# The order of work at the head of a fused retention and gMLP kernel, and where its constants are made

## The chip, the cores and the metric

The kernel runs on one core of a Trainium2 chip. The metric is the device time of one execution in microseconds (us), as the median of several runs. The profile is that of one further execution, taken by the hardware profiler. The engines are named as the profile names them: PE is TensorE (matmuls and transposes; PEld its weight loads), DVE is VectorE, ACT is ScalarE, POOL is GpSimd, SP is SyncE, which here only issues DMAs.

## The reference

Eight sequences b of 576 positions, eight heads of 64. First a retention layer (attention without softmax, with a decay by distance), then a gated MLP in which positions are mixed by a 576 x 576 matrix:

```python
# retention
scores = q @ k.transpose(0, 1, 3, 2) / sqrt(64)
gamma = 1 - 2.0 ** (-5 - arange(8))                    # one decay for each head
Dmat = where(rel >= 0, gamma[:, None, None] ** rel, 0)  # rel = row position - column position
x = (scores * Dmat) @ v                                # -> [8, 576, 512], heads side by side
# gMLP
h = gelu_tanh(x @ w_in)                                # w_in: 512 x 1024
u, v = h[..., :512], h[..., 512:]
v_n = (v - mean(v)) / sqrt(var(v) + 1e-6) * g_ln
v_s = einsum('ts,bsd->btd', w_sg, v_n) + b_sg[None, :, None]
out = x + (u * v_s) @ w_out                            # w_out: 512 x 512
```

Inputs and output are float32 in the chip's main memory.

## The kernel before

**Blocks.** The decay of a head factors into a power of gamma at the row times one at the column (`gq`, `gk`), so q and k are scaled by tables and the mask is only causal. Retention then runs in chunks with a running state for each sequence. The work is cut into 18 blocks j. Blocks 0 and 9 hold the first 64 positions of four sequences each (two chunks of 128 rows, named MID in the second stage); every other block holds 256 positions of one sequence, two to a sequence (1 and 2 for sequence 0, 3 and 4 for sequence 1, and so on). `load(j)` issues the DMAs of k, q and v of a block: four pieces of 128 KB each for blocks 0 and 9, one DMA of 512 KB each for the others, on SyncE's queue (a few pieces of block 0 on ScalarE's). They go into a pool of three buffers.

**Units of a block.** `cast(j, part, engine)` scales and rounds k, q or v to bf16. `T(j, part)` transposes k or q on TensorE; `turn(j, part)` does that by a DMA on SyncE's queue, which in the main loop is how q gets transposed. `Sc` makes scores, which VectorE masks; `Z` and `firsts` make the running states; `inter` and `intra` add up the retention of a block, which ScalarE (or VectorE) copies out as `xT`. `V(j, c)` makes the v half of the gMLP for a chunk, gelu on ScalarE, and in the head hands its statistics out as four steps: `stats_of` (VectorE), `pow_of` (GpSimd, the power -0.5 of the variance), `cen_of` (VectorE) and `norm_of` (ScalarE, which writes `vn`). `U(j, c)` makes the u half, gelu on ScalarE. `W(b, c, half)` mixes positions, with five matmuls against the transposed `w_sg`, and VectorE multiplies by u. `O` is the output projection with its store.

**How b_sg is added.** The rows of a MID chunk leave half of the 128 partitions of each operand unused. `vnm`, the normed rows of MID, has 1.0 in that half, and `wL` has three rows there that hold b_sg, split into three bf16 parts by `split_b`; `place_b(e)` copies them in with three DMAs of 1.1 KB, and `clear_wL` zeroes the rest. `fill_consts` and `fill_first` write the 1.0s, on GpSimd: for one of its three buffers in the head, for the other two in the loop at block 5.

**Order.** The order is written out by hand, and each engine takes its instructions strictly in that order; waits between engines come from the data. Lines 657 to 782 are the head: blocks 0 to 2 and the setting up of the weights (`w_in` in two halves, cast in pieces on GpSimd and ScalarE; `load_w` for `w_sg` and `w_out` on GpSimd's DMA queue; `build_wT`, which transposes `w_sg` on TensorE and copies it out on VectorE), with `spin(n)`, n matmuls on zeros that keep TensorE's clock up. From line 788 on a loop runs over blocks 3 to 17: at block j it finishes block j (`quarters`, which also makes the scores of block j + 1), casts block j + 3, transposes block j + 2, loads block j + 4, and runs W and O units of finished sequences in between. Steps put off with `later` run some units on.

**SyncE's queue in the loop.** At block j there stand on it, in order, `more(q)` (q of block j + 4) and `turn(j + 2, "q")`, then k and v of block j + 4, with the stores of O units where these fall. Up to block 5 `more(q)` comes first, from block 6 on the transpose.

The lines that the steps below touch: 93 to 138 (set up, first loads), 161 to 187 (constants and b), 189 to 194 (loads of `w_sg`), 196 to 210 (`build_wT`), 254 to 271 (`cast`), 502 to 534 (the steps of V), 657 to 782 (head), 788 to 839 (loop).

Of the kernel before, what the change touches and what calls it, by code (L numbers as in the profile page):

```python
# [15 lines left out]
Alu = mybir.AluOpType  # L16
# [3 lines left out]
def kernel(  # L20
# [123 lines left out]
    def build_masks():  # L144
        nc.vector.tensor_copy(rel[:].rearrange("p a (b t) -> p a b t", b=2), rel_i[:])
        nc.vector.tensor_scalar(rel[64:], rel[64:], 128.0, None, op0=Alu.add)
        for n in range(2):
            nc.vector.tensor_scalar(mask[n][:], rel[:], 0.0, None, op0=Alu.is_ge)
        for c in range(2):
            nc.vector.memset(mask[1][64 * c:64 * c + 32].rearrange("p a (b t) -> p a b t", b=2)[:, :, :, 32:], 0.0)  # L150
# [10 lines left out]
    def clear_wL():  # L161
        nc.gpsimd.memset(wL[0][64:], 0.0)
        nc.gpsimd.memset(wL[1][:64], 0.0)
        nc.gpsimd.memset(wnat[:, :, 0:64], 0.0)
# [8 lines left out]
                rest = left  # L173

    def fill_consts():
        for x in (1, 2):
            nc.gpsimd.memset(vnm[x][0][64:], 1.0)
            nc.gpsimd.memset(vnm[x][1][:64], 1.0)

    def fill_first():  # L180
        nc.gpsimd.memset(vnm[0][0][64:], 1.0)
        nc.gpsimd.memset(vnm[0][1][:64], 1.0)

    def place_b(e):
        for n in range(3):
            r = 64 * (1 - e) + n
            nc.gpsimd.dma_start(wL[e][r:r + 1, :], bp[:SB * 2 - 1, n, :] if e else bp[1:, n, :])

    def load_w(j):
        if j == SB:  # L190
# [29 lines left out]
    def spin(n):  # L220
        for _ in range(n):
            nc.tensor.matmul(idle[:], fill[:, :128], fill[:], start=True, stop=True)
# [177 lines left out]
    def Z(j, c):  # L400
        weave(z_steps(j, c))
# [89 lines left out]
    def V(j, c, wait=(2, 5)):  # L491
        p, m = chunk(j, c)
        hv = psD.tile([128, F2], F32, name="hv", tag="d")
        for kk in range(KK):
            nc.tensor.matmul(hv[:], xT(p, m)[:, kk], w_in[:, kk, F2:],  # L495
                             start=(kk == 0), stop=(kk == KK - 1))
        vg = vgp.tile([128, F2], F32, name="vg")
        nc.scalar.activation(vg[:], hv[:], Act.Gelu_apprx_tanh)  # L498

        st = both_of.setdefault(j, {}) if wait else {}  # L500
        k, n = (c, 2) if wait else (0, 1)

        def power():
            nc.gpsimd.tensor_tensor(st["rs"][:], st["rs"][:], mhalf[:, :n], op=Alu.pow)  # L504

        def stats():
            bst = w3.tile([128, 6], F32, name="bst")
            nc.vector.bn_stats(bst[:], vg[:])  # L508
            if not k:
                st.update(mv=w3.tile([128, n, 2], F32, name="mv"), rs=w3.tile([128, n], F32, name="rs"))  # L510
            nc.vector.bn_aggr(st["mv"][:, k], bst[:])
            if k == n - 1:
                nc.vector.tensor_scalar(st["rs"][:], st["mv"][:, :, 1], 1e-6, None, op0=Alu.add)  # L513
            if wait:
                if k:
                    power()
                centre()

        def centre():
            vc = w2.tile([128, F2], F32, name="vc", bufs=3)  # L520
            nc.vector.scalar_tensor_tensor(vc[:], vg[:], st["mv"][:, k, 0:1], g_bc[:], op0=Alu.subtract, op1=Alu.mult)  # L521
            st[k, "vc"] = vc

        def norm():
            rs, vc = st["rs"][:, k:k + 1], st[k, "vc"]
            if m == MID:
                for e in range(2):
                    half = slice(64 * e, 64 * e + 64)
                    nc.scalar.mul(vnm[p % 3][e][half], vc[half], rs[half])
                vns[p, m] = vnm[p % 3]  # L530
            else:
                vn = vnp.tile([128, F2], BF, name="vn")
                nc.scalar.mul(vn[:], vc[:], rs)  # L533
                vns[p, m] = [vn, vn]

        if wait:
            later(wait[0], stats)
            st[c] = norm
            if c:
                late = late_of.get(j, 1)  # L540
                later(wait[1] + late, st[0])
                later(wait[1] + late + 1, st[1])
        else:
            parts = stats, power, centre, norm
            for d, f in zip((stats_of, pow_of, cen_of, norm_of), parts):
                d[2 * j + c] = f
        tick()
# [109 lines left out]
    HEAD = 3  # L657
    spin(16)
    build_masks()
    cast(0, "k", nc.vector)  # L660
    T(0, "k")
    spin(2)
    cast(0, "q", nc.vector)
    T(0, "q")
    spin(3)
    cast(0, "v", nc.gpsimd)
    clear_wL()
    Sc(0, 0)
    Sc(0, 1)
    firsts(0)  # L670
    nc.gpsimd.tensor_copy(w_in[:, :2, F2:], w_stage[1][:, :2])
    nc.scalar.copy(w_in[:, 2:, F2:], w_stage[1][:, 2:])
    cast(1, "k", nc.gpsimd)
    spin(9)
    inter(0)
    intra(0)
    load(3)
    cast(1, "q", nc.vector)
    build_g()
    V(0, 0, None)  # L680
    V(0, 1, None)
    T(1, "k")
    T(1, "q")
    split_b()
    cast(1, "v", nc.gpsimd)
    spin(2)
    Sc(1, 0)
    Z(1, 0)
    stats_of[0]()
    cast(2, "k", nc.gpsimd)  # L690
    spin(2)
    inter(1)
    Sc(1, 1)
    Z(1, 1)
    load(4)
    cast(2, "q", nc.vector)
    spin(4)
    T(2, "k")
    spin(3)
    intra(1)  # L700
    T(2, "q")
    cen_of[0]()
    for j in range(SB):
        load_w(j)
    pow_of[0]()
    fill_first()
    cast(2, "v", nc.gpsimd)
    nc.gpsimd.tensor_copy(w_in[:, :, :256], w_stage[0][:, :, :256])
    V(1, 0, None)
    Sc(2, 0)  # L710
    V(1, 1, None)
    Z(2, 0)
    nc.scalar.copy(w_in[:, :, 256:F2], w_stage[0][:, :, 256:])
    inter(2)
    place_b(0)
    Sc(2, 1)
    firsts(1)
    start_state(1)
    wb = ["L0", "L1"] + list(range(SB - 1))
    U(0, 0)  # L720
    stats_of[2]()
    pow_of[2]()
    cen_of[2]()
    U(0, 1)
    stats_of[3]()
    pow_of[3]()
    intra(2)
    cen_of[3]()
    place_b(1)
    U(1, 0)  # L730
    V(2, 0, None)
    norm_of[2]()
    V(2, 1, None)
    load(5)
    norm_of[0]()
    stats_of[4]()
    pow_of[4]()
    cen_of[4]()
    build_wT(wb[0])
    U(1, 1)  # L740
    stats_of[5]()
    pow_of[5]()
    build_wT(wb[1])
    norm_of[3]()
    cen_of[5]()
    U(2, 0)
    cast(3, "k", nc.gpsimd)
    build_wT(wb[2])
    norm_of[4]()
    build_wT(wb[3])  # L750
    norm_of[5]()
    build_wT(wb[4])
    build_wT(wb[5])
    cast(3, "q", nc.vector)
    release(2)
    run(1)
    T(3, "k")
    cast(3, "v", nc.scalar)
    run(1)
    T(3, "q")  # L760
    U(2, 1)
    cast(4, "k", nc.gpsimd)
    cast(4, "q", nc.gpsimd)
    cast(4, "v", nc.scalar)
# [7 lines left out]
    T(4, "k")  # L772
    run(1)
    T(4, "q")
    run(1)
    cast(5, "q", nc.gpsimd)
    cast(5, "k", nc.gpsimd)
    cast(5, "v", nc.gpsimd)
# [9 lines left out]
    for j in range(HEAD, NB):  # L788
        nx = j + 1 < NB
        slots = where[share.get(j, 6)] if nx else (3, 0, 1, 1)  # L790
        more = (lambda *p: load(j + 4, p)) if j + 4 < NB else (lambda *p: None)
        if j < 6:
            more(q)
        if j + 2 < NB:
            turn(j + 2, "q")
            if j + 5 >= NB or j in EXTRA:
                turn(j + 2, "k")
        if j >= 6:
            more(q)

        if nx:
            quarters(j)
# [24 lines left out]
        if j + 3 < NB:  # L827
            cast(j + 3, "k", nc.gpsimd)
            cast(j + 3, "v", nc.gpsimd)
        if j == HEAD + 2:  # L830
            fill_consts()
        U(j, 1)
        if nx and place(j)[1] is not None and place(j)[2] == (place(j)[1] + 1 == GB) and place(j)[1] + 1 < B:
            start_state(place(j)[1] + 1)
# [41 lines left out]
```

## Time and profile before

| | |
|---|---|
| median of 3 runs | 219.12 us (218.86 to 222.0) |
| the profiled execution's own time | 219.96 us |
| its span, first to last instruction | 218.1 us |
| mean granted TensorE clock | 0.989 of full speed |
| busy share of the span | PE 92%, DVE 75%, ACT 59%, POOL 59% |
| DMA | 47.47 MB, 218 GB/s over the span |

The span is some 2 us shorter than the execution's own time, which also has start and end in it. A row of the profile in order of time gives the start in us, the length in us, the engine (with a q where it is the sequencer that issues a DMA), the line of the kernel, the operation, the tiles written and read, and how many instructions it stands for; in brackets stands how long the engine was idle before and what ended that. A row of a group gives the count, the busy time in us with the mean of one in ns, and the idle time before them. A DMA's row gives KB and the us from its issue to its landing.

### The profile page before, as it was taken

How to read it: one execution, taken by the hardware profiler on the slowest of the kernel's cores; microseconds unless marked ns; L12 is line 12 of the kernel's file. 1: busy time of each engine (PE TensorE's matmuls, PEld its weight loads, DVE VectorE, ACT ScalarE, POOL GpSimd, SP SyncE). 2: the span in 40 equal slices, each digit the busy share in tenths (PEclk: the TensorE clock that was granted, in tenths of full speed). 3: DMA queues.
4: the chain of work that ended last, by engine and by line, in shares of the span. 5: the costliest groups of instructions: out<-in, count | busy, mean ns of one | idle time of the engine just before them, and what ended most of it. 6: DMA issues, size and time to landing. Idle time of an engine off the chain costs nothing.

```text
span 218.1 us, 7982 instructions
## 1 busy us (share of the span) xinstructions
PE 201.0 (92%) x3403; PEld 142.5 (65%) x3433; DVE 164.1 (75%) x342; ACT 128.3 (59%) x221; POOL 128.9 (59%) x146
## 2 busy tenths in 40 slices
PE   7797989899979999899899999999999999999990
PEld 2344567568747687658586876668776876667650
DVE  5557869989957989856856779657866997968771
ACT  4354468564749777476568595777557374655100
POOL 5087978869895959856465747692957532111000
PEclk9999999979999999999999999999999999999998
DMA  6999999949999999999948999899999895532335
GB/s 155 254 312 291 335 243 286 290 109 295 198 278 248 282 213 182 278 182 340 247 111 131 335 242 216 196 267 315 198 276 201 201 125 136 155 101 48 144 93 200
DMA packets 88180, 47.47 MB, mean 218 GB/s; under 512 B 26000, under 2 KB 82640, under 8 KB 88144
## 3 DMA queue, kind: packets, MB, share of 16 engines
q1 hardware_dynamic: 85440, 45.10, 92.2%
q0 software_dynamic: 1472, 1.20, 3.3%
q10 hardware_dynamic: 1232, 0.66, 1.3%
q8 instruction: 27, 0.44, 0.9%
q14 instruction: 9, 0.07, 0.1%
HBM read 32.79 MB, written 9.44 MB: 194 GB/s over the span
## 4 chain that ended last, share of the span: by engine, by line
PE 63%; DVE 7%; DMA 4%; POOL 2%; issue 2%; ACT 1%; DVEq 0%; POOLq 0%; ACTq 0%
PE wp L586 15%; PE op L608 13%; PE hv L495 11%; PE hu L563 10%; DMA qT<-qb 4%; PE ot L479 3%; PE sc L345 3%; PE ot L437 2%; PE op L612 2%; PE tp L279 2%; DVE vc L521 2%; DVE qb L270 1%; DVE bst L508 1%; POOL rs L504 1%; POOL qb L270 1%
## 5 line engine op out<-in xcount | busy, mean ns | idle before, releaser
L349 DVE TENSOR_TENSOR ret<-sc,mask 128x512 bf16<-128x512 f32 x72 | 46.1, 682 | 14.6 <-PE sc L345 8.1
L504 POOL TENSOR_TENSOR rs<-rs,mhalf 128x2 f32<-128x2 f32 (+1 forms) x21 | 20.7, 987 | 55.5 <-DVE rs L513 55.3
L586 PE MATMUL wp<-wT,vn 128*128 128x288 bf16 x256 | 42.4, 289 | 0.9 <-DVE wT L252 0.9
L608 PE MATMUL op<-w_out,gT 128*128 128x512 bf16 (+1 forms) x131 | 34.8, 373 | 0.8
L563 PEld LDWEIGHTS <-w_in 128*128 128x128 bf16 x576 | 34.1, 98 | 1.9
L588 DVE TENSOR_TENSOR gT<-wp,uT 128x288 bf16<-128x288 f32 x64 | 27.5, 450 | 9.4 <-PE wp L586 9.0
L495 PE MATMUL hv<-w_in,xT 128*128 128x512 bf16 x119 | 31.9, 379 | 1.9 <-issue 1.0
L563 PE MATMUL hu<-xT,w_in 128*128 128x128 bf16 x512 | 33.6, 219 | 0.0
L508 DVE BATCH_NORM_STATS2 bst<-vg 128x6 f32<-128x512 f32 x36 | 24.7, 687 | 10.9 <-ACT vg L498 10.9
L270 POOL TENSOR_TENSOR kb<-qk,gk 128x1024 bf16<-128x1024 f32 x16 | 31.3, 1961 | 1.5 <-DMA qk<-in_k_dram 1.5
L498 ACT ACTIVATE vg<-hv 128x512 f32<-128x512 f32 x36 | 21.4, 597 | 14.7 <-PE hv L495 14.6
L586 PEld LDWEIGHTS <-vn 128*128 128x128 bf16 x256 | 24.1, 99 | 8.5 <-ACT vn L533 1.3
L521 DVE SCALAR_TENSOR_TENSOR vc<-vg,mv,g_bc 128x512 f32<-128x512 f32 x36 | 29.0, 805 | 0.6
L252 ACT CAST xT<-ot 128x512 bf16<-128x512 f32 x30 | 20.2, 741 | 14.2 <-PE ot L479 14.2
L270 POOL TENSOR_TENSOR qb<-qk,gq 128x1024 bf16<-128x1024 f32 x14 | 28.0, 1999 | 0.0
L566 ACT ACTIVATE uT<-hu 128x512 bf16<-128x512 f32 x32 | 19.1, 603 | 11.0 <-PE hu L563 11.0
L533 ACT ACTIVATE vn<-vc,rs 128x512 bf16<-128x512 f32 x32 | 22.4, 722 | 4.5 <-POOL rs L504 4.3
L608 PEld LDWEIGHTS <-gT 128*128 128x128 bf16 x148 | 13.3, 98 | 11.1
L495 PEld LDWEIGHTS <-xT 128*128 128x128 bf16 x128 | 11.8, 98 | 12.3 <-issue 1.3
L345 PE MATMUL sc<-qT,kT 64*64 64x128 bf16 x576 | 16.2, 219 | 2.7 <-DMA qT<-qb 1.6
L252 ACT COPY kT<-tp 128x1024 bf16<-128x1024 bf16 x15 | 15.2, 1010 | 6.0 <-PE tp L279 6.0
L586 PE MATMUL wp<-wL,vnm 128*128 128x288 bf16 x64 | 18.5, 289 | 0.0
(115 smaller groups left out, 294.2 us busy)
## 6 DMA issues: line engine op xcount, KB each, us to landing
qk<-in_k_dram SPq DMA_DIRECT2D x16, 512.0 KB, 6.7
qk<-in_q_dram SPq DMA_DIRECT2D x16, 512.0 KB, 7.0
vf<-in_v_dram SPq DMA_DIRECT2D x16, 512.0 KB, 7.5
out_dram<-ob SPq DMA_DIRECT2D x20, 256.0 KB, 4.7
out_dram<-obs SPq DMA_DIRECT2D x11, 256.0 KB, 2.4
wst<-in_moe_w_in_dram SPq DMA_DIRECT2D x2, 1024.0 KB, 7.4
vf<-in_v_dram SPq DMA_DIRECT2D x8, 128.0 KB, 4.7
out_dram<-ob SPq DMA_DIRECT2D x8, 128.0 KB, 2.8
```

What stands on the lines that cost most here:

```text
L252: (eng.copy if eng is nc.scalar else eng.tensor_copy)(o, i)
L270: eng.tensor_tensor(o, src, tab[:, kind].rearrange("p a h -> p h a").unsqueeze(3).to_broadcast([128, H, 2, D]), op=Alu.mult)
L345: nc.tensor.matmul(sc[r][cc, x, a, :], kT[rr, a, kk, cc], qT[rr, :, kk, cc], start=True, stop=True, skip_group_check=True)
L349: nc.vector.tensor_tensor(s["ret"][:, r, 2 * g:2 * g + 2], sc[r][:], mask[1 if place(j)[1] is None else 0][:].unsqueeze(1).to_broadcast([1 ...
L495: nc.tensor.matmul(hv[:], xT(p, m)[:, kk], w_in[:, kk, F2:], start=(kk == 0), stop=(kk == KK - 1))
L504: nc.gpsimd.tensor_tensor(st["rs"][:], st["rs"][:], mhalf[:, :n], op=Alu.pow)
L508: nc.vector.bn_stats(bst[:], vg[:])
L521: nc.vector.scalar_tensor_tensor(vc[:], vg[:], st["mv"][:, k, 0:1], g_bc[:], op0=Alu.subtract, op1=Alu.mult)
L563: nc.tensor.matmul(hu[:, c, :], w_in[:, kk, 128 * c:128 * c + 128], xT(p, m)[:, kk], start=(kk == 0), stop=(kk == KK - 1), skip_group_chec ...
L586: nc.tensor.matmul(ps[:], vns[p, m][e][:, 128 * c:128 * c + 128], w, start=(x == 0), stop=(x == SB - 1))
L588: nc.vector.tensor_tensor(gTs[p][:, c, col:col + HS], ps[:], uTs[b][:, c, half * HS:half * HS + HS], op=Alu.mult)
L608: nc.tensor.matmul(op[:], gTs[p][:, c, r], w_out[:, c, f], start=(c == 0), stop=(xn is not None and c == KK - 1), skip_group_check=True)
```

## The change

The head is put in another order and some work goes to other engines. In the order of the diff:

- `fill_consts` writes the 1.0s of all three buffers of `vnm` at once, on VectorE, ahead of the first cast; `fill_first` and the call in the loop go. `clear_wL` comes ahead of the casts, `split_b` ahead of the cast of v of block 0, both still on GpSimd. `place_b` issues its six DMAs on SyncE's queue, between the loads of blocks 3 and 4, not on GpSimd's.
- In `norm`, for MID chunks of the loop (block 9), one of the two halves is scaled on GpSimd, not on ScalarE.
- The numbers of idle matmuls (`spin`) are 34 in all, not 41.
- `build_g`, the scores and inner part of block 1, its V units, and the steps of the statistics come at other places; the loads of `w_sg` are issued in two parts, with the cast of v of block 2 between; the U units come at other places among the builds of the transposed `w_sg`.
- k of block 3 is cast on GpSimd further ahead, and q of block 3 on GpSimd, not on VectorE, also further ahead.
- U of block 2, second chunk, comes ahead of the first W unit, and one of the W units of the head moves to an earlier place.
- In the loop the transpose of q of block j + 2 comes ahead of the load of q of block j + 4 for blocks 3 to 5 too.

```diff
--- before.py
+++ after.py
@@ -173,18 +173,14 @@
                 rest = left
 
     def fill_consts():
-        for x in (1, 2):
-            nc.gpsimd.memset(vnm[x][0][64:], 1.0)
-            nc.gpsimd.memset(vnm[x][1][:64], 1.0)
-
-    def fill_first():
-        nc.gpsimd.memset(vnm[0][0][64:], 1.0)
-        nc.gpsimd.memset(vnm[0][1][:64], 1.0)
+        for x in vnm:
+            nc.vector.memset(x[0][64:], 1.0)
+            nc.vector.memset(x[1][:64], 1.0)
 
     def place_b(e):
         for n in range(3):
             r = 64 * (1 - e) + n
-            nc.gpsimd.dma_start(wL[e][r:r + 1, :], bp[:SB * 2 - 1, n, :] if e else bp[1:, n, :])
+            nc.sync.dma_start(wL[e][r:r + 1, :], bp[:SB * 2 - 1, n, :] if e else bp[1:, n, :])
 
     def load_w(j):
         if j == SB:
@@ -526,7 +522,10 @@
             if m == MID:
                 for e in range(2):
                     half = slice(64 * e, 64 * e + 64)
-                    nc.scalar.mul(vnm[p % 3][e][half], vc[half], rs[half])
+                    if e and wait:
+                        nc.gpsimd.tensor_scalar(vnm[p % 3][e][half], vc[half], rs[half], None, op0=Alu.mult)
+                    else:
+                        nc.scalar.mul(vnm[p % 3][e][half], vc[half], rs[half])
                 vns[p, m] = vnm[p % 3]
             else:
                 vn = vnp.tile([128, F2], BF, name="vn")
@@ -657,108 +656,112 @@
     HEAD = 3
     spin(16)
     build_masks()
+    clear_wL()
+    fill_consts()
     cast(0, "k", nc.vector)
     T(0, "k")
     spin(2)
     cast(0, "q", nc.vector)
     T(0, "q")
     spin(3)
+    split_b()
     cast(0, "v", nc.gpsimd)
-    clear_wL()
     Sc(0, 0)
     Sc(0, 1)
     firsts(0)
     nc.gpsimd.tensor_copy(w_in[:, :2, F2:], w_stage[1][:, :2])
     nc.scalar.copy(w_in[:, 2:, F2:], w_stage[1][:, 2:])
     cast(1, "k", nc.gpsimd)
-    spin(9)
+    spin(4)
+    build_g()
     inter(0)
     intra(0)
+    spin(3)
     load(3)
+    place_b(0)
+    place_b(1)
     cast(1, "q", nc.vector)
-    build_g()
     V(0, 0, None)
     V(0, 1, None)
     T(1, "k")
+    stats_of[0]()
     T(1, "q")
-    split_b()
     cast(1, "v", nc.gpsimd)
     spin(2)
     Sc(1, 0)
+    Sc(1, 1)
     Z(1, 0)
-    stats_of[0]()
+    pow_of[0]()
     cast(2, "k", nc.gpsimd)
+    spin(1)
+    inter(1)
+    Z(1, 1)
     spin(2)
-    inter(1)
-    Sc(1, 1)
-    Z(1, 1)
+    cen_of[0]()
+    intra(1)
     load(4)
     cast(2, "q", nc.vector)
-    spin(4)
+    spin(1)
     T(2, "k")
-    spin(3)
-    intra(1)
+    V(1, 0, None)
+    norm_of[0]()
+    for j in range(2):
+        load_w(j)
+    cast(2, "v", nc.gpsimd)
+    for j in range(2, SB):
+        load_w(j)
     T(2, "q")
-    cen_of[0]()
-    for j in range(SB):
-        load_w(j)
-    pow_of[0]()
-    fill_first()
-    cast(2, "v", nc.gpsimd)
+    Z(2, 0)
+    stats_of[2]()
+    V(1, 1, None)
     nc.gpsimd.tensor_copy(w_in[:, :, :256], w_stage[0][:, :, :256])
-    V(1, 0, None)
+    nc.scalar.copy(w_in[:, :, 256:F2], w_stage[0][:, :, 256:])
+    pow_of[2]()
     Sc(2, 0)
-    V(1, 1, None)
-    Z(2, 0)
-    nc.scalar.copy(w_in[:, :, 256:F2], w_stage[0][:, :, 256:])
+    Sc(2, 1)
     inter(2)
-    place_b(0)
-    Sc(2, 1)
     firsts(1)
     start_state(1)
     wb = ["L0", "L1"] + list(range(SB - 1))
     U(0, 0)
-    stats_of[2]()
-    pow_of[2]()
+    intra(2)
     cen_of[2]()
+    norm_of[2]()
     U(0, 1)
     stats_of[3]()
     pow_of[3]()
-    intra(2)
+    V(2, 0, None)
     cen_of[3]()
-    place_b(1)
-    U(1, 0)
-    V(2, 0, None)
-    norm_of[2]()
     V(2, 1, None)
     load(5)
-    norm_of[0]()
+    norm_of[3]()
     stats_of[4]()
+    cast(3, "k", nc.gpsimd)
     pow_of[4]()
+    U(1, 0)
     cen_of[4]()
-    build_wT(wb[0])
-    U(1, 1)
     stats_of[5]()
     pow_of[5]()
+    norm_of[4]()
+    U(1, 1)
+    cen_of[5]()
+    cast(3, "q", nc.gpsimd)
+    build_wT(wb[0])
+    norm_of[5]()
+    U(2, 0)
     build_wT(wb[1])
-    norm_of[3]()
-    cen_of[5]()
-    U(2, 0)
-    cast(3, "k", nc.gpsimd)
     build_wT(wb[2])
-    norm_of[4]()
     build_wT(wb[3])
-    norm_of[5]()
+    U(2, 1)
     build_wT(wb[4])
     build_wT(wb[5])
-    cast(3, "q", nc.vector)
     release(2)
     run(1)
     T(3, "k")
     cast(3, "v", nc.scalar)
     run(1)
     T(3, "q")
-    U(2, 1)
+    run(1)
     cast(4, "k", nc.gpsimd)
     cast(4, "q", nc.gpsimd)
     cast(4, "v", nc.scalar)
@@ -772,7 +775,6 @@
     T(4, "k")
     run(1)
     T(4, "q")
-    run(1)
     cast(5, "q", nc.gpsimd)
     cast(5, "k", nc.gpsimd)
     cast(5, "v", nc.gpsimd)
@@ -789,14 +791,11 @@
         nx = j + 1 < NB
         slots = where[share.get(j, 6)] if nx else (3, 0, 1, 1)
         more = (lambda *p: load(j + 4, p)) if j + 4 < NB else (lambda *p: None)
-        if j < 6:
-            more(q)
         if j + 2 < NB:
             turn(j + 2, "q")
             if j + 5 >= NB or j in EXTRA:
                 turn(j + 2, "k")
-        if j >= 6:
-            more(q)
+        more(q)
 
         if nx:
             quarters(j)
@@ -827,8 +826,6 @@
         if j + 3 < NB:
             cast(j + 3, "k", nc.gpsimd)
             cast(j + 3, "v", nc.gpsimd)
-        if j == HEAD + 2:
-            fill_consts()
         U(j, 1)
         if nx and place(j)[1] is not None and place(j)[2] == (place(j)[1] + 1 == GB) and place(j)[1] + 1 < B:
             start_state(place(j)[1] + 1)
```

## The prediction

> **What bounds the kernel now.** I read the shares of the page first, then the chain that ended last, then TensorE's waits, and last the 30 us around the place where they point.
>
> The page's table of engines, its TensorE row:
>
> ```profile
> PE 201.0 (92%) x3403; PEld 142.5 (65%) x3433; DVE 164.1 (75%) x342; ACT 128.3 (59%) x221; POOL 128.9 (59%) x146
> ```
>
> The chain in order of time (start, us, what), from where block 5 begins to matter, and one unit of each later kind:
>
> ```profile
> 42.39 2.81 DVE qb L270
> ...
> 46.28 0.89 PE hu L563 x16
> 47.17 0.40 PE sc L345 x16
> ...
> 50.45 1.94 POOL qb L270
> ...
> 52.67 8.80 DMA qT<-qb
> 61.52 0.63 PE sc L345 x30
> ...
> 65.77 0.45 PE tp L279 x8
> ...
> 73.08 0.86 PE hv L495 x4
> ...
> 76.90 0.61 PE wp L586 x5
> ```
>
> The longest of TensorE's waits after 60 us (who <- whom: us in total, times, longest):
>
> ```profile
> PE sc L345 <- DMA qT<-qb: 1.6, 1, 1.6
> ```
>
> The reader is to see two stages. From 61.52 on nearly every step of the chain is TensorE's. Before it the head is held by other things: the cast of q of block 3 on VectorE, that of q of block 5 on GpSimd, and the DMA that transposes the latter, for which TensorE waits 1.6 us. So the change, nearly all of it in the head, is worth what the score matmuls of block 5 (61.52) gain, as long as the later stream keeps up.
>
> What the DMA does meanwhile: SyncE's queue in order of time (start, length, what), and four stretches (length, then busy us of PE, PEld, DVE, ACT and POOL, granted clock, DMA share, GB/s):
>
> ```profile
> 21.86 2.00 SPq L88 DMA_DIRECT2D qk<-in_q_dram  x1
> 23.95 4.94 SPq L88 DMA_DIRECT2D vf<-in_v_dram  x1
> 29.00 3.40 SPq L88 DMA_DIRECT2D qk<-in_k_dram  x1
> ...
> 39.50 1.75 SPq L88 DMA_DIRECT2D vf<-in_v_dram  x1
> 47.01 0.37 SPq L88 DMA_DIRECT2D qk<-in_k_dram  x1
> ...
> 49.43 3.14 SPq L88 DMA_DIRECT2D qk<-in_q_dram  x1
> ```
>
> ```profile
> 40.00:44.00 4.00, 3.09 (x22) 2.02 (x23) 3.97 (x10) 1.76 (x4) 4.00 (x2) 0.84 1.19 294
> 44.00:49.00 5.00, 4.46 (x82) 3.34 (x81) 4.05 (x7) 3.02 (x4) 2.98 (x2) 0.78 0.40 93
> 42.70:46.20 3.50, 2.96 (x24) 2.16 (x22) 3.22 (x3) 1.96 (x2) 3.50 (x2) 0.51 0.88 212
> 59.90:63.40 3.50, 1.84 (x84) 1.48 (x83) 1.64 (x4) 0.67 (x2) 3.50 (x4) 1.00 1.08 265
> ```
>
> The DMA moves 294 GB/s up to 44 and then 93 for 5 us, because the loads of block 6 wait for casts until 47.01: 5 x (294 - 93) / 294 = 3.4 us of data are not moved. The transpose of block 5, issued at 52.67 and landed at 61.47, lies behind this hole and behind q of block 7 (49.43).
>
> **The change part by part.** All is timed in the profiled execution: span 218.1 us, own time 219.96; the median of the runs, 219.12, is 0.84 below that.
>
> *Constants on VectorE.* Six fills of 64x512 with 1.0 go in ahead of the first cast. VectorE's last row before the gap there, its cast of q, and the groups of two fills:
>
> ```profile
> 3.58 0.27 DVE L150 MEMSET mask<- 32x64 uint32 x2
> ...
> 7.71 1.23 DVE L270 TENSOR_TENSOR qb<-qk,gq 128x1024 bf16<-128x1024 f32 x1 [1.11 <-DMA qk<-in_q_dram]
> ```
>
> ```profile
> L103 DVE MEMSET fill<- 128x256 uint32 x1 | 0.3, 272 | 0.9 <-PEq L860 0.9
> L181 POOL MEMSET vnm<- 64x512 bf16 x1 | 0.5, 519 | 0.1
> ```
>
> The lower end is 6 x 0.27 = 1.6 us (512 elements written as 256 words, as the zero fill was), the upper 6 x 0.52 = 3.1, GpSimd's row for this very shape and value. I take 3.1, the nearer row. VectorE is free at 3.85 + 3.1 = 7.0, and with two casts of 1.23 q is done at 9.5 instead of 8.94: 0.5 us late. A later wait, for v of block 1, hides it:
>
> ```profile
> 20.52 0.44 PE L370 MATMUL zf<-vb,kb 64*64 64x64 bf16 x16 [0.89 <-POOL vb L252]
> ```
>
> It is 0.89 us long, so the fills cost nothing; without that cover, 0.5. [...]
>
> *Work on b and the order of the middle.* GpSimd gets rid of memsets, of the split of b and of six DMA issues; block 1's inner part and V units come ahead of block 2's; q of block 3 is cast on GpSimd. First the low half of w_in, as SyncE issues it, its landing (KB, us) and ScalarE's cast; then TensorE's first U unit, four of its builds of transposed weights, the loop's first matmul and the next block's:
>
> ```profile
> 19.23 1.74 SPq L132 DMA_DIRECT2D wst<-in_moe_w_in_dram  x1
> ```
>
> ```profile
> wst<-in_moe_w_in_dram SPq DMA_DIRECT2D x1, 1024.0 KB, 8.3
> ```
>
> ```profile
> 29.42 1.05 ACT L713 CAST w_in<-wst 128x1024 bf16<-128x1024 f32 x1
> 30.68 1.96 PE L563 MATMUL hu<-xm,w_in 128*128 128x128 bf16 x32
> 38.68 1.90 PE L201 MATMUL wtp<-ident,wnat 128*128 128x128 bf16 x20
> 51.60 0.44 PE L370 MATMUL zf<-vlead,klead 32*64 32x64 bf16 x32
> 59.28 0.63 PE L437 MATMUL ot<-qT,zb 64*64 64x128 bf16 x16
> ```
>
> The weights land at 27.5 and could be cast by 28.6; ScalarE has V units and block 0's scaling before it, so I put the first U at 29.2 (bounds 28.6 and 30.68). From there to the loop TensorE took 51.60 - 30.68 = 20.9 us, for six U (0.89), two V (0.86), six builds (0.48), four transposes (0.45), six W (0.61), and some 1.7 of scores, states and inner part (by the 0.40 row): 16.9. The other 4.0 are waits for VectorE, whose 2.81 us cast now leaves it, and half clock. I leave 0.9 of the 4.0 (bounds 0.4 and 3): the loop starts at 29.2 + 17.8 = 47.0, and block 5's scores, 7.7 later, are ready at 54.7 (56.8 with the 3).
>
> *The DMAs of b on SyncE's queue.* This part costs. One of SyncE's waits, and landings (KB, us) of q and v of block 3, v of block 5 and k of block 6:
>
> ```profile
> SPq L84 <- DMA qk<-in_k_dram: 1.7, 2, 1.4
> ```
>
> ```profile
> qk<-in_q_dram SPq DMA_DIRECT2D x1, 512.0 KB, 12.4
> ...
> vf<-in_v_dram SPq DMA_DIRECT2D x1, 512.0 KB, 12.6
> ...
> vf<-in_v_dram SPq DMA_DIRECT2D x1, 512.0 KB, 7.5
> ...
> qk<-in_k_dram SPq DMA_DIRECT2D x1, 512.0 KB, 5.7
> ```
>
> Pieces of v of block 0 waited for pieces of k that they don't touch. They are the ninth DMA of the hardware queues and on; I read it as each taking the semaphore of the eighth before it. With six small DMAs between loads 3 and 4, the eighth before k of block 4 is q of block 3, and before q of block 4 it is v of block 3. So k is issued at 21.86 + 12.4 = 34.3, not 29.00, and q at 23.95 + 12.6 = 36.6; behind them on SyncE stand all loads of blocks 4 to 6. A load of 512 KB is 1.8 us of data at 294 GB/s, and k of block 6, into an idle DMA, took 5.7: up to 3.9 beside its data, of which I take 3.4, as q ran beside it. At each stop only one load is still to move, so each leaves a hole of 3.4 - 1.8 = 1.6 us. Upper end, two of 2.1: 4.2. Lower end nothing, if the loads of w_sg, three of which GpSimd now issues behind the cast of v, fill them. I take one of the two, 1.6.
>
> *Block 6 sooner, transposes first.* The hole of 3.4 goes if GpSimd has cast q of blocks 3 and 4 before block 5's data ends: q of block 4 lands at 36.6 + 3.4 + 1.8 = 41.8 and is cast, 1.94 later, by 43.8, while v of block 5, landed at 47.0 now, comes at 48.6. And block 5's transpose goes ahead of q of block 7, 1.8 of data. Behind it on SyncE stand q, k and v of block 7, whose first cast is
>
> ```profile
> 63.85 1.93 POOL L270 TENSOR_TENSOR qb<-qk,gq 128x1024 bf16<-128x1024 f32 x1
> ```
>
> at 63.85, or 60.2 when 3.6 sooner. The transpose lands at 61.47 - 3.4 - 1.8 + 1.6 = 57.9, and q of block 7 at 59.7, in time by 0.5.
>
> So TensorE is ready at 54.7 and waits until 57.9: the transpose sets the gain, 3.6 us. The wait of 3.2 has a price. The clock stood at 0.51 from 42.7 to 46.2, after thin work and no long gap, while the 1.6 us of waiting at 59.9 left it at 1.00. So between 0 and 3.5 x 0.49 = 1.7; I take the middle, 0.8, as the rows point opposite ways. [...]
>
> *Rest.* In block 9 two scalings of 64x512 go to GpSimd, 0.5 (its memset of that shape) to 1.0 (half of 1.94) each; I take 1.0, hidden by the units before W needs them, at worst 2. Four memsets leave GpSimd at block 5, off the chain; seven fewer idle matmuls and the DMA issues moved off GpSimd change nothing here, since the DMA sets the pace.
>
> Sum: 3.6 - 0.8 = 2.8. 219.96 - 2.8 = 217.2 profiled, 219.1 - 2.8 = **216.3** for the median.
>
> **Rivals.** *TensorE sets the pace.* If the data of w_sg fills the holes (lower end 0), the transpose lands near 56 and the scores gain 5.3 without half clock: 213.8. For it: 54.7 rests on measured units. Against: the semaphore wait.
>
> *The gain doesn't come.* The holes are 4.2 long: 3.4 + 1.8 - 4.2 = 1.0, less 0.8 of clock: 218.9. For it: 5.7 us of k of block 6. Against: only a full hole at both stops gives it.
>
> *Slower: SyncE stands at the transpose.* Put in front of loads, it holds them until its cast is done, and GpSimd now casts five times in a row up to q of block 5. That q lands one load before v, 46.8, and is cast by 48.8. But beside VectorE's cast one took more:
>
> ```profile
> 44.07 2.91 POOL L270 TENSOR_TENSOR qb<-qk,gq 128x1024 bf16<-128x1024 f32 x1
> ```
>
> Five at 2.91 are 4.8 more: 53.6, 0.9 after today's issue, with the DMA dry behind block 6 and 1.7 of half clock: 2.6 slower, 221.7. It decides from 52.67 on. Against: the cast that collided is the one that leaves VectorE.
>
> **How the numbers follow.** Forecast 0.52; TensorE's pace 0.20; no gain 0.18; slower 0.10. The forecast's own range is 214.6 to 218.2. With parts of the cases on both sides, 213.2 to 219.8 leaves out the slower case and the far edges, 2 in 10. A measurement of this kernel tells about 2%, 4.4 us, from no change. Faster than 214.7: most of the second case and the forecast's low edge, 0.25. Slower than 223.5: the edge of the last, 0.05. Within: 0.70.
>
> **What would show it.** After: the hole near 46 gone; k of block 4 issued near 34; the first U near 29, the loop near 47; block 5's scores near 58 behind 3 us of waiting for the transpose. A loop start after 49, a transpose landing before 56 or after 60, or new waits past block 6 would make the prediction wrong.

## The result and the profile after

The changed kernel takes 218.25 us (median of 22 executions, 215.51 to 220.66); the kernel before, on the same chip at the same time, 220.03 (22, 218.24 to 222.0). The ratio is **0.9874**, with a 95% interval of 0.9845 to 0.9904: 1.3% faster, less than the 2% that I called the limit of what a measurement of this kernel tells. By the medians the gain is 1.8 us, 0.8%. The forecast was 216.3 us, a gain of 2.8 or 1.3%. Single executions of one of these kernels lie up to 3.6% apart (two outliers aside, one of 701.52 us of the shifted run on b and one of 236.16 of the kernel before), so ratios here are formed of those within 1.5% of its fastest, and medians of all of them.

The profiled execution took 219.85 us, more than the median. From its page, the engines and the shares of the chain that ended last:

```profile
PE 200.6 (92%) x3426; PEld 141.1 (65%) x3426; DVE 167.8 (77%) x347; ACT 126.7 (58%) x219; POOL 127.8 (59%) x137
...
PE 68%; POOL 4%; issue 3%; DVE 2%; ACT 1%; DVEq 0%; POOLq 0%
```

The first experiment, the changed kernel once more, gave a ratio of 0.9897 (0.9862 to 0.9933; 12 executions, median 217.83) and a profiled execution of 217.2 us, span 215.4. It is nearer to the median, and I read the change from it. The same rows of its page, and its queue of instruction reads (reads, MB, share), which matters further down:

```profile
PE 197.5 (92%) x3397; PEld 140.9 (65%) x3426; DVE 164.1 (76%) x347; ACT 126.8 (59%) x219; POOL 127.6 (59%) x137
...
q8 instruction: 27, 0.44, 0.9%
...
PE 64%; DMA 9%; SPq 2%; POOL 1%; issue 1%; DVE 0%; DVEq 0%; POOLq 0%
```

> The changed kernel once more, for a second profile and as the base of the three beside it. Theory A (the stream of loads paces the head): 1.0 to 1.5% below the kernel before; in its profile k of block 4 is issued six issues of the small DMAs late, near 36, the DMA moves little from 35 to 39 instead of from 45 to 49, and TensorE waits some 1 to 3 us between 50 and 61 for work that hangs on q of block 5 or 6. Theory B (TensorE and GpSimd pace the head by their own work): the same time, but the waits between 50 and 61 are for casts whose data has long landed.

SyncE's queue in order of time in this execution (start, length, what):

```profile
23.61 3.42 SPq L88 DMA_DIRECT2D vf<-in_v_dram  x1
27.08 7.58 SPq L183 DMA_DIRECT2D wL<-bp  x6
34.78 0.40 SPq L88 DMA_DIRECT2D qk<-in_k_dram  x1
35.69 0.37 SPq L88 DMA_DIRECT2D qk<-in_q_dram  x1
...
47.40 1.62 SPq L88 DMA_DIRECT2D vf<-in_v_dram  x1
50.67 4.37 SPq L290 DMA_TRANSPOSE qT<-qb  x1
55.10 1.13 SPq L88 DMA_DIRECT2D qk<-in_q_dram  x1
```

Stretches of it, as before (the granted clock is the third number from the end, GB/s the last):

```profile
33.00:37.00 4.00, 3.95 (x48) 2.91 (x47) 3.64 (x9) 3.28 (x6) 2.35 (x2) 1.00 0.42 105
40.00:44.00 4.00, 3.28 (x35) 2.24 (x32) 3.11 (x12) 2.13 (x4) 4.00 (x4) 1.00 1.19 288
42.70:46.20 3.50, 3.33 (x62) 2.78 (x62) 2.38 (x6) 2.64 (x3) 3.22 (x2) 1.00 1.16 286
44.00:49.00 5.00, 4.83 (x92) 3.86 (x90) 4.71 (x10) 3.17 (x4) 3.40 (x5) 1.00 1.14 287
```

TensorE in order of time: the loop's first matmul, the scores of block 5 and the first output projection behind them:

```profile
49.25 0.44 PE L366 MATMUL zf<-vlead,klead 32*64 32x64 bf16 x32
...
59.92 0.64 PE L341 MATMUL sc<-qT,kT 64*64 64x128 bf16 x32 [2.04 <-DMA qT<-qb]
...
61.19 1.04 PE L607 MATMUL op<-w_out,gT 128*128 128x512 bf16 x3
```

The reader is to see four things. The dry stretch at 44 to 49 us is gone: 287 GB/s where there were 93. The six small DMAs of b hold SyncE from 27.08 to 34.66, k of block 4 goes out at 34.78 instead of 29.00, and the DMA runs thin from 33 to 37 us (105 GB/s; in the execution of 219.85 us k went out at 36.90, and from 35 to 39 the DMA moved 86). The clock stays at 1.00 where it had fallen to 0.51. And the scores of block 5 start 1.6 us sooner (59.92 for 61.52), still behind a wait for the transpose, now of 2.04 us. At the end of the span the gain is 2.7. In the execution of 219.85 us the scores start at 60.89, 0.6 sooner than before.

### The profile page after: what moved, and what is told of

Read it like the earlier page. It is cut to its first block, busy times and chain, and to the rows that moved or that the text cites. A ratio compares the mean times of both kernels' runs of the same rounds, so it can differ in the third digit from the quotient of the medians.

```text
span 218.1 us, 8001 instructions
## 1 busy us (share of the span) xinstructions
PE 200.6 (92%) x3426; PEld 141.1 (65%) x3426; DVE 167.8 (77%) x347; ACT 126.7 (58%) x219; POOL 127.8 (59%) x137
## 4 chain that ended last, share of the span: by engine, by line
PE 68%; POOL 4%; issue 3%; DVE 2%; ACT 1%; DVEq 0%; POOLq 0%
PE wp L585 17%; PE op L607 13%; PE hu L562 11%; PE hv L491 11%; PE sc L341 4%; PE ot L475 3%; PE ot L433 3%; PE tp L275 2%; PE op L611 2%; POOL qb L266 2%; POOL rs L500 1%; PE zp L366 1%; DVE qT L248 1%; DVE gT L587 1%; POOL vb L248 0%
## 5 line engine op out<-in xcount | busy, mean ns | idle before, releaser
L585 PE MATMUL wp<-wT,vn 128*128 128x288 bf16 x256 | 41.9, 286 | 0.7 <-DVE wT L248 0.7
L587 DVE TENSOR_TENSOR gT<-wp,uT 128x288 bf16<-128x288 f32 x64 | 28.0, 452 | 11.5 <-PE wp L585 10.6
L607 PE MATMUL op<-w_out,gT 128*128 128x512 bf16 (+1 forms) x148 | 36.1, 374 | 0.0
L266 POOL TENSOR_TENSOR qb<-qk,gq 128x1024 bf16<-128x1024 f32 x15 | 28.9, 1930 | 4.6 <-PE hu L562 4.3
L517 DVE SCALAR_TENSOR_TENSOR vc<-vg,mv,g_bc 128x512 f32<-128x512 f32 x36 | 30.5, 846 | 0.5
L341 PE MATMUL sc<-qT,kT 64*64 64x128 bf16 x576 | 15.7, 219 | 2.6 <-issue 1.3
```

What stands on the lines that cost most here:

```text
L266: eng.tensor_tensor(o, src, tab[:, kind].rearrange("p a h -> p h a").unsqueeze(3).to_broadcast([128, H, 2, D]), op=Alu.mult)
L341: nc.tensor.matmul(sc[r][cc, x, a, :], kT[rr, a, kk, cc], qT[rr, :, kk, cc], start=True, stop=True, skip_group_check=True)
L585: nc.tensor.matmul(ps[:], vns[p, m][e][:, 128 * c:128 * c + 128], w, start=(x == 0), stop=(x == SB - 1))
L587: nc.vector.tensor_tensor(gTs[p][:, c, col:col + HS], ps[:], uTs[b][:, c, half * HS:half * HS + HS], op=Alu.mult)
L607: nc.tensor.matmul(op[:], gTs[p][:, c, r], w_out[:, c, f], start=(c == 0), stop=(xn is not None and c == KK - 1), skip_group_check=True)
```

## The experiments

| what was run | median, us (executions) | ratio to the kernel before |
|---|---|---|
| changed kernel again | 217.83 (12) | 0.9897 (0.9862 to 0.9933) |
| b's DMAs on GpSimd's queue | 217.11 (6) | 0.9866 (0.9814 to 0.9917) |
| the same again | 217.57 (6) | 0.9899 (0.9861 to 0.9937) |
| new head, loads ahead of transposes | 221.1 (6) | none: the executions lie too far apart |
| the same again | 219.85 (12) | 0.9902 (0.9857 to 0.9947) |
| old head, transposes ahead of loads | 219.93 (12) | 0.9999 (0.9967 to 1.0031) |
| cast of q of block 3 back on VectorE | 218.3 (6) | 0.9892 (0.983 to 0.9954) |
| fills issued twice | 220.5 (12) | 1.0028 (0.9995 to 1.0062) |
| fills spread over VectorE's waits | 219.94 (6) | 0.9874 (0.9808 to 0.994) |
| b on GpSimd, 64 instructions more | 219.77 (12) | 0.9969 (0.9932 to 1.0007) |
| changed kernel, 64 instructions more | 220.29 (12) | 0.9978 (0.9931 to 1.0024) |
| kernel before, 64 instructions more | 221.83 (6) | 1.0113 (1.0056 to 1.017) |

The kernel before stood beside them at 219.35 to 220.25 us.

**The DMAs of b.** My theory was that the stream of loads paces the head, and that b on SyncE costs it a hole.

```diff
-            nc.sync.dma_start(wL[e][r:r + 1, :], ...)
+            nc.gpsimd.dma_start(wL[e][r:r + 1, :], ...)
...
     cast(1, "k", nc.gpsimd)
+    place_b(0)
+    place_b(1)
```

> The six DMAs of b go out on GpSimd's queue right behind the cast of k of block 1, where GpSimd was idle for 3 us, instead of on SyncE's between loads 3 and 4. Theory A: k of block 4 is issued near 29.5, the thin stretch at 35 to 39 is gone, the loads of blocks 4 to 6 land 2 to 3 us sooner, and the kernel is 1.5 to 2.8 us faster than the changed one. Theory B: the thin stretch goes too, but the time stays within 0.7 us of the changed one.

SyncE's queue with b off it, and the stretch in which the DMA ran thin:

```profile
27.55 3.05 SPq L88 DMA_DIRECT2D qk<-in_k_dram  x1
...
49.85 1.41 SPq L290 DMA_TRANSPOSE qT<-qb  x1
```

```profile
33.00:37.00 4.00, 4.00 (x58) 3.36 (x57) 3.64 (x8) 3.12 (x6) 3.16 (x3) 1.00 1.17 301
```

The hole is real: 301 GB/s instead of 105, so b on SyncE leaves 4 x (301 - 105) / 301 = 2.6 us of data unmoved. TensorE's rows: the first output projection, and the inner part of block 5 (in brackets how long it was idle before, and what ended that):

```profile
58.55 0.82 PE L607 MATMUL op<-w_out,gT 128*128 128x512 bf16 x2
...
67.81 0.46 PE L475 MATMUL ot<-ret,vb 64*64 64x128 bf16 x18
70.83 0.36 PE L475 MATMUL ot<-ret,vb 64*64 64x128 bf16 x12 [2.56 <-issue]
```

The projection starts at 58.55 instead of 61.19, with no wait for the transpose left. Yet the whole is not faster than the change: TensorE stood 2.56 us in the middle of 32 equal matmuls, and no engine or DMA of data ended that. What did begin at 68.1 to 68.3 us is one packet on the queue of instruction reads (packets, MB, share of 16 engines in these 0.2 us):

```profile
q8 instruction: 1, 0.02, 37.0%
```

37% of 16 engines in 0.2 us is 0.37 x 16 x 0.2 = 1.2 us for this read of 16 KB (by the page above, 0.44 MB in 27 reads). So I ran it again, to see whether the stop is chance.

> The first experiment on b once more, unchanged (the six small DMAs of b on GpSimd's queue behind the cast of k of block 1, SyncE's queue free of them). Its profile showed the loop 0.8 us and the first O unit 2.6 us sooner than the changed kernel, and then 2.56 us in which TensorE stood in the middle of block 5's inner part, with nothing that it waited for, while a 16 KB read of the instruction queue began at 68.18. Theory: the stop is a late read of TensorE's own instructions, by chance of how the reads fall among the loads; then it need not come again, and if it does not, the profiled time is 2 to 3 us lower than 217.8. Rival: something in the kernel's order makes it, and it stands in this profile too, at the same instruction. Median 216.5 to 217.5 either way.

It came back, behind the same 18 matmuls:

```profile
71.85 0.36 PE L475 MATMUL ot<-ret,vb 64*64 64x128 bf16 x12 [2.02 <-issue]
```

So the rival holds, that something in the order makes it. It is not b: with b on SyncE's queue the same 12 matmuls come behind a stop of 2.23 us in the run with spread fills below, of 1.20 with the fills doubled and of 1.14 with the cast of block 3 back on VectorE, and in the changed kernel once more behind none. (This execution took 220.44 us, with two more stops later; the median of the six is 217.57.) In these two traces moving b off SyncE buys 1 to 2.6 us at block 5 and loses it before 73 us; the ratios, 0.9866 and 0.9899 for 0.9897, show no gain.

**The order in the loop.** First the new head with the old order, then the old head with the new order:

```diff
+        if j < 6:
+            more(q)
         if j + 2 < NB:
             turn(j + 2, "q")
             ...
-        more(q)
+        if j >= 6:
+            more(q)
```

> The changed kernel with the load of q of block j + 4 again ahead of the transpose of block j + 2 for blocks 3 to 5. Theory A as predicted (the transpose of block 5 sets the gain): it lands 1.8 us later and the kernel is 1 to 1.8 us slower than the changed one. Theory A2 (the stream paces, but by q of block 6, whose cast GpSimd waits for with the states of block 4 behind it): q of block 6 goes out ahead of both, so the time stays within 0.5 us. Theory B: within 0.5 us too, with the transpose landing before TensorE needs it.

> The kernel before with one edit: the block loop issues the transposes of block j+2 ahead of q of block j+4, for all blocks. The head stays as it was. My theory (the order in the loop carries most of the gain, the head little) expects the transpose of block 5 some 1.8 us sooner (issued near 49.5 to 51 instead of 52.67), the wait of 1.6 us for it gone or under 0.5, and 1 to 2.5 us less than the kernel before in the median. The rival that the order helps only behind the new head (where GpSimd has cast q of block 5 early) expects no difference (within 0.7 us), because in the kernel before that cast ends at 52.4 and the transpose could not be issued sooner anyway.

> The changed kernel with the loads of the next blocks ahead of the transposes in the loop again, as in the first call, where it gave 221.1 us from six runs far apart (216.66 to 222.43). With the order alone worth nothing in front of the old head, the new head alone should say whether both are needed. Theory: the two belong together, since the transpose can only go first when the cast of q in front of it is done early; then this gives 219 to 221, no gain against the kernel before. Rival: the head carries the gain and the six runs were unlucky; then 217.5 to 218.5.

New head, old order: SyncE's rows, GpSimd's cast of q of block 5, and TensorE's wait, from the first of the two runs; and the wait in the second:

```profile
47.14 3.23 SPq L88 DMA_DIRECT2D vf<-in_v_dram  x1
50.47 1.66 SPq L88 DMA_DIRECT2D qk<-in_q_dram  x1
52.23 5.86 SPq L290 DMA_TRANSPOSE qT<-qb  x1
```

```profile
47.91 1.95 POOL L266 TENSOR_TENSOR qb<-qk,gq 128x1024 bf16<-128x1024 f32 x1
```

```profile
58.27 0.58 PE L433 MATMUL ot<-qT,zb 64*64 64x128 bf16 x14 [0.73 <-POOL zb L389]
60.91 0.74 PE L341 MATMUL sc<-qT,kT 64*64 64x128 bf16 x32 [2.07 <-DMA qT<-qb]
```

```profile
64.64 1.04 PE L341 MATMUL sc<-qT,kT 64*64 64x128 bf16 x32 [4.81 <-DMA qT<-qb]
```

The cast is done at 49.86, but the transpose goes out at 52.23. SyncE was held by v of block 6 until 50.37, so 1.8 of these 2.4 us are q of block 7 (50.47 to 52.23). Behind the wait the clock falls, for 3.5 us, to 0.51:

```profile
61.30:64.80 3.50, 3.28 (x73) 2.23 (x63) 2.81 (x5) 1.33 (x2) 3.50 (x5) 0.51 1.21 291
```

Old head, new order: SyncE's transpose, GpSimd's cast, and TensorE's scores of block 5.

```profile
51.63 2.06 SPq L294 DMA_TRANSPOSE qT<-qb  x1
```

```profile
49.66 1.95 POOL L270 TENSOR_TENSOR qb<-qk,gq 128x1024 bf16<-128x1024 f32 x1
```

```profile
58.98 0.64 PE L345 MATMUL sc<-qT,kT 64*64 64x128 bf16 x32
```

Here the transpose goes out as the cast ends (51.61), and cannot go sooner; in the kernel before it went 0.3 us behind that cast's end (52.39, 52.67). But it lands 7.3 us later and not 8.8, now that q of block 7 is not ahead of it, and TensorE's wait is gone: the scores start at 58.98, 2.5 sooner than before (0.8 of this is a loop that starts at 50.81 for 51.60) and 0.9 sooner than in the changed kernel. So in this trace, of an execution of 218.28 us, the order alone did open something. The median does not show it: 0.9999, where I had expected 1 to 2.5 us. The rival named the right time, but its reason, that the transpose could not go sooner, is not the whole of it, and where the gain of this trace goes in the other executions is not shown.

The head alone is less clear. Its best execution (216.66) comes within 1.2 us of the changed kernel's best (215.5), but the median of all 18 is 220.2, against 218.1 for the 34 of the changed kernel. Twelve of the 18 ran on a chip on which the kernel before took 220.25, and the changed kernel with spread fills 219.94, so part of this distance can be the chip. That the two parts need each other, the head so that GpSimd finishes the cast sooner and the order so that the transpose can use it, is how I read the medians. It is argued, not shown: the ratio of 0.9902 speaks against it, and so does the trace of the order alone.

**The cast of q of block 3 on GpSimd.**

```diff
-    cast(3, "q", nc.gpsimd)
...
+    cast(3, "q", nc.vector)
     release(2)
```

> The changed kernel with q of block 3 cast on VectorE again, in its old place ahead of the first W unit. Theory A: the loop starts 2 us later, but TensorE then waits less for the stream, so the time is within 0.7 us of the changed one. Theory B: TensorE is 2 us late for good, 1.5 to 2.5 us slower.

0.9892, the same as the change. Its loop starts at 49.75, 0.5 us later and not 2, and GpSimd's cast of q of block 4 takes 2.82 us beside VectorE's, as 2.91 in the kernel before, against 1.93 in the changed kernel. Within the new head this part is worth nothing that can be measured.

**The fills.**

```diff
     fill_consts()
+    fill_consts()
     cast(0, "k", nc.vector)
```

> The changed kernel with its six fills of 64x512 on VectorE issued twice: 3.7 us more ahead of the first casts. The fills already hold the cast of k of block 0 from 5.4 to 7.5 and the scores of block 0 from 10.2 to 11.1. My step (the loads pace the head, and a later wait hides a late start) expects less than 1.5 us of it at the first O unit and in the median. The rival that the head is paced by its own work (TensorE, VectorE) expects 3 to 3.7 us more, and then the fills of the change cost 0.9 us too.

```diff
+    fill_consts(0)
     cast(0, "k", nc.vector)
+    fill_consts(1)
...
     Sc(0, 1)
+    fill_consts(2)
```

> The changed kernel, but its six fills stand on VectorE where that engine waits anyway: two ahead of the cast of k of block 0, two between that cast and the cast of q, two behind the scores of block 0. If TensorE's own work paces the head (as the doubled fills say, which cost 2.9 us of 3.7), the scores of block 0 start 0.9 us sooner (10.2 instead of 11.1) and the median falls by 0.6 to 1.0 us against the changed kernel, to about 0.986 of the kernel before. If a later wait hides it, as my prediction put it, the median stays (0.989 to 0.990).

VectorE in order of time, in the changed kernel (first and last fill, casts of k and q of block 0 and of q of block 1):

```profile
3.98 0.48 DVE L177 MEMSET vnm<- 64x512 bf16 x1
...
7.12 0.48 DVE L178 MEMSET vnm<- 64x512 bf16 x1
7.53 1.15 DVE L266 TENSOR_TENSOR klead<-qk,gk 128x1024 bf16<-128x1024 f32 x1
8.61 1.20 DVE L266 TENSOR_TENSOR qb<-qk,gq 128x1024 bf16<-128x1024 f32 x1
...
17.25 1.39 DVE L266 TENSOR_TENSOR qb<-qk,gq 128x1024 bf16<-128x1024 f32 x1 [1.17 <-DMA qk<-in_q_dram]
```

With the fills spread, the cast of k starts at 5.23, and that of q of block 1 is

```profile
17.27 1.40 DVE L265 TENSOR_TENSOR qb<-qk,gq 128x1024 bf16<-128x1024 f32 x1 [1.99 <-DMA qk<-in_q_dram]
```

and with the fills doubled

```profile
21.21 1.20 DVE L266 TENSOR_TENSOR qb<-qk,gq 128x1024 bf16<-128x1024 f32 x1
```

The fills hold the first cast from 5.23 to 7.53, but q of block 1 only lands at 17.2: VectorE's wait for it is 1.99 us with the fills out of the way and 1.17 with them in it, and the cast starts at the same time. So they are hidden, by the loads, and spreading them shows no gain (0.9874, where the change has 0.9874 and 0.9897). Six more are not hidden. They put the cast of k at 11.52, 4.0 later, and TensorE, which stands until then, starts slowly:

```profile
12.72 1.03 PE L275 MATMUL tp<-ident,klead 128*128 128x128 bf16 x8 [5.04 <-DVE klead L266]
```

1.03 us for eight transposes that take 0.62 in the changed kernel, where the idle matmuls end 2.50 us ahead of them and not 5.04, and 0.62 in the kernel before, where they run up to them. The wait for q of block 1 is used up, its cast comes 4.0 late too, and the whole takes 1.3% or 2.9 us more (1.0028 against 0.9897). My expectation of under 1.5 was wrong: the loads cover about a microsecond of a late start, not four.

**TensorE's instruction reads.** 27 reads for 3397 + 3426 recorded instructions of TensorE are one for 253; the 256 in the texts of the runs below is an estimate, no closer than this count. If the stops come from reads that are late at such a border, shifting the borders must shift the stops.

```diff
-    spin(16)
+    spin(13)
+    for _ in range(35):
+        nc.tensor.matmul(idle[:, :1], fill[:, :128], fill[:, :1], ...)
```

(In the run on b the 16 stay and 32 are added; both make 64 instructions more, a matmul and its weight load each.)

> As the run on b, with 32 matmuls of one column in the first idle time of TensorE (64 more instructions, about 2 us of time in which TensorE waits for its first data). This shifts where the 16 KB borders of TensorE's instruction stream fall in the work by 64 of 256 instructions. If the borders' place decides (a border in front of the run of small matmuls of a block's scores and inner part), the stop of 2.56 us goes or moves by tens of instructions, and the median changes by 1 us or more, up or down. If the reads are late by chance of the DMA's load alone, the median stays within 0.7 us of the run on b. The added matmuls themselves cost nothing, or up to 0.5 us.

> The changed kernel with 3 of the 16 first idle matmuls replaced by 35 of one column: 64 more instructions for TensorE, no work of it later than before. The 16 KB borders of its instruction stream then fall 64 of 256 instructions elsewhere in the work. If the place of these borders is worth a microsecond or more (it gave 2 us more in the run on b), the median moves by 1 us or more, most likely up, since the present place has no long stop in the profile at 217.2. If not, it stays within 0.6 us of 217.8.

> The kernel before with the same exchange of 3 idle matmuls for 35 of one column, 64 more instructions. It tells whether part of the 2.3 us between the two kernels is only where the 16 KB borders fall. If the kernel before lies badly, it gains 1 us or more (its profile has a stop of 1.0 at 107.2 behind a late read); if the gain of the change is of its order of work, the kernel before stays within 0.6 us of 219.4 or gets slower.

All three got slower than the same kernel without the shift: by 0.7% (b on GpSimd), 0.8% (changed kernel) and 1.1% (before), each give or take 0.6%. TensorE's longest idle time behind 65 us, in the run on b, in the changed kernel and in the kernel before, each shifted:

```profile
105.42 0.22 PE L366 MATMUL zf<-vlead,klead 32*64 32x64 bf16 x4 [3.30 <-issue]
```

```profile
105.12 0.23 PE L366 MATMUL zf<-vlead,klead 32*64 32x64 bf16 x5 [3.27 <-issue]
```

```profile
106.16 0.29 PE L370 MATMUL zf<-vlead,klead 32*64 32x64 bf16 x12 [2.77 <-issue]
```

The same matmuls, a new stop of 2.8 to 3.3 us in each, and none of this length there in the profiles without the shift. The read that belongs to the second began between 102.40 and 102.50:

```profile
q8 instruction: 1, 0.02, 74.8%
```

0.748 x 16 x 0.1 = 1.2 us, so it had landed at 103.65, and TensorE went on at 105.12, 1.5 later; in the run on b the read of 68.2 landed at 69.4 and TensorE went on 1.4 later. The stop at block 5's inner part is gone from the shifted run on b. Where the borders fall is thus worth nearly as much here as the whole change. It does not explain the change, though: shifted against shifted the ratio is 0.9978 / 1.0113 = 0.987 (about 0.979 to 0.994, from the two intervals), as without the shift.

## Why the prediction was right, and where it was not

The total was right by the ratio, 1.3% for 1.3%, and by the median, 218.25 us for 216.3, it lies within the range. Its parts were mostly right in their direction, but several were wrong in size, in ways that cancelled, so it is in part luck that the totals agree. Two of my own signs of being wrong came up: the loop starts after 49, at 49.25, and in the execution of 219.85 us the transpose landed after 60, at 60.4 (51.82 + 8.6).

- *What bounds.* Block 5's scores and the transpose in front of them were the point to look at: the wait is there before and after, and in the traces of the runs that take it away or lengthen it the first output projection moves by microseconds. The medians do not follow: order alone takes the wait away and is no faster.
- *Hole of 3.4 us at 46.* Gone, as said.
- *b on SyncE: the term that was mis-sized.* k of block 4 was put at 34.3 and went at 34.78, for a reason that I had not given: the six small DMAs take SyncE 7.58 us between them, and k goes out as the last is issued. q of block 4 did wait as I had described: it goes out at 35.69, as v of block 3 lands (23.61 + 12.1). The hole was put at 1.6 us (0 to 4.2) and is 2.6, so that of the 3.4 won at 46 only 0.8 was left. That the whole kernel would be faster without it, which the sum implies, is not seen: in the two traces the time comes back as stops of TensorE.
- *Landing of the transpose: the step that failed.* I took the landing and subtracted data, 3.4 and 1.8, and added 1.6: 57.9. It landed at 59.9, 9.2 after its issue. With a hole of 2.6 the sum gives 58.9. The other 1.0 shows in the time from issue to landing: 8.8 us before, 9.2 now, although q of block 7 no longer lies in front. The load that does, v of block 6, was to land sooner by the same sum; it landed at 58.4, before at 57.7 (48.04 + 9.7). Its row and the transpose's in the changed kernel:

```profile
vf<-in_v_dram SPq DMA_DIRECT2D x1, 512.0 KB, 11.0
...
qT<-qb SPq DMA_TRANSPOSE x1, 9.2
```

  Why it came no sooner is open. The transpose also has to wait for its cast, which stands in my slower rival, put at 48.8 there, but in no term of the sum. It ends at 50.64, 1.8 us sooner than before:

```profile
48.69 1.95 POOL L266 TENSOR_TENSOR qb<-qk,gq 128x1024 bf16<-128x1024 f32 x1
...
62.08 1.92 POOL L266 TENSOR_TENSOR qb<-qk,gq 128x1024 bf16<-128x1024 f32 x1
```

  The first of these rows is that cast (52.39 was its end before), the transpose goes at 50.67, and the scores start at 59.92. The gain there is 1.6, not 3.6. The cast alone would have allowed nearly what I forecast: in the run on b, where v of block 6 had landed at 52.4, the transpose took 7.4 us from its issue, and 50.67 + 7.4 is 58.1.
- *TensorE ready at 54.7.* It was ready at 57.9 (59.92 - 2.04). The first U came at 29.89 for 29.2, the loop at 49.25 for 47.0. My list of units adds up to 17.1 us and not 16.9, and from the loop to the scores I took 7.7 where the kernel before has 8.3 (51.60 to 61.52 - 1.61). That limit was not the one that counted, since the transpose was later still.
- *Half clock, 0.8.* It cost nothing: 1.00 behind the wait of 2.04 us. The middle between two rows that point opposite ways was a value that no trace here shows: in this one it is nothing, in the run with the old order, by the same estimate, 3.5 x 0.49 = 1.7. Behind waits and stops of TensorE the traces show both half clock and full. The granted clock was 0.51 behind 0.73 and 2.07 us of them in the run with the old order, and 0.51 from 71.6 to 75.1 behind the 2.56 of the run on b. It was 1.00 from 71.8 to 75.3 behind the 2.02 of that run's second trace, and from 106.1 to 109.6 behind the 2.77 of the shifted kernel before. What decides between the two is not shown.
- *Fills.* Put at 3.1 us, they took 3.6 (six of 0.48, one each 0.63), and were hidden as said, though the wait that hides them is VectorE's for q of block 1, ahead of the one that I named.
- *Rest, 0.* Between block 5 and the end another 1.1 us were gained (1.6 at 59.92, 2.7 at the end), for which I had no step. Single executions differ by more than that, and no run took it apart: it stays open. The scalings on GpSimd took 1.7 us each, not 1.0:

```profile
125.53 3.38 POOL L526 TENSOR_SCALAR vnm<-vc,rs 64x512 bf16<-64x512 f32 x2
```

So 1.6 + 0 + 1.1 stands where 3.6 - 0.8 stood. Of the rivals, TensorE does not set the pace at block 5, as it waits there. SyncE does stand at the transpose, from 49.02 to 50.67, and q of block 7 goes out at 55.10 instead of 49.43, but its cast, the second row above, still comes 1.8 us sooner than before (62.08 for 63.85). That the gain does not come is what the order alone does by its median; for the head alone it is open.

## What to carry to other kernels

When a transfer is late, price both what lets it be issued and the data in front of it, and measure a hole in the stream over all of its length: the same hole is 2.6 us from 33 to 37 and would be read as 1.0 from 35 to 39 (205 GB/s for 276). A wait that goes in one trace is not yet a gain: the order alone took one of 1.6 us away and left the median where it was, so compare many executions, of the parts of a change and of the whole. In a kernel whose TensorE is 92% busy, a gain in the middle can be lost again to stops that I put down to the instruction stream (2.56 and 2.02 us in the two traces of the run on b), so shift it by some instructions before believing a difference of one per cent.

## What the hardware did that was not expected

- In these traces instructions are read in pieces of 16 KB while the kernel runs (27 reads, 0.44 MB, in the changed kernel once more), and TensorE stops where one is late: for 2.56 us in the run on b, 2.02 in its second trace, and 3.30, 3.27 and 2.77 in the three shifted runs. In the two stops whose read I worked out, those of 2.56 and 3.27, it went on 1.4 and 1.5 us after the read had landed; all five stand in runs of small matmuls. That these reads are TensorE's own, and that the stops are waits for them, is inferred: from one read per 253 of its instructions, and from the stops that moved with the shift in all three kernels. Why a read starts late is open.
- Six DMAs of 1.1 KB from SBUF to SBUF kept SyncE's queue for 7.58 us in the changed kernel once more, and for 7.53 and 5.17 in the two runs with the old order.
